# A feed-forward after attention in one 64x64 array shape: contraction halves on two row tiles, one nine steps behind the other

## The chip, the cores and the metric

The kernel runs on one core of one Trainium2 chip. The metric is the time of one execution on the device in microseconds (us), as the median of several executions. Most executions of one kernel agree within about 1%. Every ratio below is the mean time of one kernel's runs over that of the other's runs of the same rounds, so it is not quite the ratio of the medians that are quoted. The span of a profile is about 1.7 us shorter than the time of the same execution.

Names of engines in the profile: PE is the TensorE matmul, PEld its weight load, DVE is VectorE, ACT is ScalarE, POOL is GpSimd, SP is SyncE.

## The reference, cut to what matters

```python
# q, k, v: (8 batches, 12 heads, 448, 64);  w_gate, w_val: (768, 1536);  w_out: (1536, 768)
scores = matmul(q, k.transpose(0, 1, 3, 2)) / sqrt(64)
attn   = maximum(scores, 0) ** 2 / 448
x      = matmul(attn, v)  ->  rows of 768 = 12 heads * 64, for 8 * 448 = 3584 tokens
out    = (maximum(x @ w_gate, 0) * (x @ w_val)) @ w_out         # float32, 3584 x 768
```

## The kernel before

Everything is written as operations with durations; a planner in the kernel orders them on each engine, mixing the attention of batch b+1 into the feed-forward of batch b. Products differ in the shape of the array that they use (a row tile is the part of the array that takes 64 of the contraction's rows, a column tile the part that gives 64 of the output's; a bank is the piece of PSUM, TensorE's output memory, into which one product adds):

- scores: contraction over 64 (the head), 128 keys out, so two heads run at once on two row tiles (64x128), and a rest of 64 keys in four tiles (64x64);
- values: contraction over 128 keys, 64 columns out, two heads at once on two column tiles (128x64), and the rest in four tiles;
- the feed-forward: full array (128x128).

```python
# scores (Part.s): j and h2 pick one of four heads, c a chunk of 128 keys
if not tail:
    for m, j in enumerate(js):
        for h2 in range(2):
            nc.tensor.matmul(half_of(h2)[:, m * n:(m + 1) * n],
                             lhsT=kq(1, j, h2, key_off(b) + c * 128, 128),
                             rhs=kq(0, j, h2, self.c0, n), start=True, stop=True)
else:
    for j, h2, half in ((0, 0, 0), (0, 1, 1), (1, 0, 1), (1, 1, 0)):      # 64x64 each
        ...
# values (Part.pv), after four 64x64 matmuls of the key rest
for j in range(2):
    for c in range(NC):
        for h2 in range(2):
            o = slice(64 * h2, 64 * h2 + 64)
            nc.tensor.matmul(x_of(o, j), lhsT=st.vv[:, 4 * g + 2 * j + h2, 1 + c, :],
                             rhs=self.at(j, c, h2), start=False, stop=(c == NC - 1))
# feed-forward, gate and value products (gv_ops): KD = 6 steps of 448 columns each
for kd in range(KD):
    nc.tensor.matmul(ps, lhsT=w[c][:, kd, o:o + 128], rhs=st.xT[:, kd, cols],
                     start=(kd == 0), stop=(kd == KD - 1))
# feed-forward, output product (ffn_ops): KF = 12 steps of 384 columns
for kf in range(KF):
    nc.tensor.matmul(loc["o"], lhsT=hs["hT"][:, kf, ti * 128:(ti + 1) * 128],
                     rhs=w_out_sb[hf][:, kf, :], start=(kf == 0), stop=(kf == KF - 1))
# attention of batches 1 to 7 goes to the planner in bursts of three products;
# the first product of a burst borrows two of the feed-forward's four PSUM banks (split)
for k0 in (0, NC):
    nb += 1
    for i in range(k0, k0 + NC):
        att.append((pt.s(i, split=i == k0), nb))
nb += 1
att.append((pt.s(pt.tail), nb))
...            # then the value product of the group before, in the same burst
```

Of the kernel before, what the change touches and what calls it, by code (L numbers as in the profile page):

```python
# [14 lines left out]
XBAR_FROM = 2  # L15

# [17 lines left out]
class Op:  # L34
    def __init__(self, engs, emit, deps=(), alloc=(), reads=(), xfer=0.0, prio=1, delay=0.0, bias=0.4):
        self.engs, self.emit = engs, emit
        self.deps, self.alloc, self.reads = list(deps), list(alloc), list(reads)
        self.xfer, self.prio, self.delay = xfer, prio, delay
        self.bias = bias
        self.lat = 1.3  # L40
        self.start = self.end = None


class Planner:
    LAT = 0.26
    NOUT = 8

    def __init__(self):
        self.t = {"POOL": 1.35}
        self.ops = []  # L50
        self.dmaq = 0.0
        self.landed = []

    def ready(self, op):
        r = 0.0
        for d in op.deps:
            if d.end is None:
                return None
            r = max(r, d.end + self.LAT + op.delay)
        need = {}  # L60
        for b in op.alloc:
            need[b.res] = need.get(b.res, 0) + 1
        for res, n in need.items():
            if len(res.free) < n:
                return None
            r = max(r, sorted(res.free)[n - 1] + self.LAT)
        return r
# [12 lines left out]
    def commit(self, op, s, e):  # L80
        op.start, op.eng = s, e
        d = op.engs[e]
        self.t[e] = s + d
        op.end = s + d
        if op.xfer:
            if e == "POOL":
                self.dmaq = max(self.dmaq, op.end + op.lat) + op.xfer
                op.end = self.dmaq + 0.7
                self.landed.append(op.end)
            else:  # L90
                op.end += 2.0 + op.xfer
        for b in op.alloc:
            b.res.free.remove(min(b.res.free))
            b.last = op.end
        for b in op.reads:
            b.readers -= 1
            b.last = max(b.last, op.end)
            if b.readers == 0:
                b.res.free.append(b.last)
        self.ops.append(op)  # L100


def plan(att, ffn, others, pool, nburst, calm):
# [9 lines left out]
    while ai < len(att) or fi < len(ffn) or pend or pi < len(pool):  # L113
# [37 lines left out]
        elif pick == "A":  # L151
# [8 lines left out]
            gap = work / max(1, left) if left > 0 and last_burst >= calm else 0.0  # L160
# [4 lines left out]
    return [P.ops[i] for i in order]  # L165
# [3 lines left out]
def kernel(  # L169
# [19 lines left out]
    P2 = 64  # L189
# [139 lines left out]

    zeros = const.tile([128, 512], BF16)  # L330
# [5 lines left out]
    def transpose_pair(b, g, j):  # L336
# [21 lines left out]
        op = Op({"PE": 0.5 if g or b else 0.95}, emit, deps=list(st.qk_op[h]) + list(st.qk_op[h + 1]) + [id_op],  # L358
# [48 lines left out]
    class Part:  # L407
# [37 lines left out]
        def s(self, i, split=False):  # L445
# [10 lines left out]
            def emit():  # L456
# [9 lines left out]
                if not tail:  # L466
                    for m, j in enumerate(js):
                        for h2 in range(2):
                            nc.tensor.matmul(half_of(h2)[:, m * n:(m + 1) * n],  # L469
                                             lhsT=kq(1, j, h2, key_off(b) + c * 128, 128),  # L470
                                             rhs=kq(0, j, h2, self.c0, n), start=True, stop=True)
                else:

                    for j, h2, half in ((0, 0, 0), (0, 1, 1), (1, 0, 1), (1, 1, 0)):
                        nc.tensor.matmul(half_of(h2)[64 * half:64 * half + 64, :n],  # L475
                                         lhsT=kq(1, j, h2, key_tail(b), P2),
                                         rhs=kq(0, j, h2, self.c0, n), start=True, stop=True)

            op = Op({"PE": (0.06 if not tail else 0.11) + ne / 2400.0}, emit, deps=[t_op[(b, 2 * g + j)] for j in js],
# [29 lines left out]
        def pv(self, split=False):  # L509
            b, g, n = self.b, self.g, self.n  # L510
# [4 lines left out]
            def emit():  # L515
                if split:
                    loc["x"] = [bank("x1_ps"), bank("x1_ps")]
                    x_of = lambda o, j: loc["x"][j][o, :n]
                else:
                    loc["x"] = bank_pair()  # L520
                    x_of = lambda o, j: loc["x"][o, j, :n]
                for j, h2, half in ((0, 0, 0), (0, 1, 1), (1, 0, 1), (1, 1, 0)):
                    p = slice(64 * half, 64 * half + 64)
                    o = slice(64 * h2, 64 * h2 + 64)
                    nc.tensor.matmul(x_of(o, j), lhsT=st.vv[p, 4 * g + 2 * j + h2, (NC + 1) * (1 - half), :],  # L525
                                     rhs=self.at_tail(h2)[p], start=True, stop=False)
                for j in range(2):
                    for c in range(NC):
                        for h2 in range(2):
                            o = slice(64 * h2, 64 * h2 + 64)  # L530
                            nc.tensor.matmul(x_of(o, j), lhsT=st.vv[:, 4 * g + 2 * j + h2, 1 + c, :],  # L531
                                             rhs=self.at(j, c, h2), start=False, stop=(c == NC - 1))

            dv = [d for h in range(4 * g, 4 * g + 4) for d in st.v_op[h]]
            op = Op({"PE": 0.2 + 7 * n / 2400.0}, emit, deps=self.sq + dv, alloc=ps, reads=[self.at_buf, st.vbuf])
# [24 lines left out]
            return op  # L560
# [3 lines left out]
    def gv_ops(b, c0, n, mf):  # L564
# [10 lines left out]
        def product(name, w):  # L575
            ps = bank(name)[:, :n]
            for kd in range(KD):
                nc.tensor.matmul(ps, lhsT=w[c][:, kd, o:o + 128], rhs=st.xT[:, kd, cols],  # L578
                                 start=(kd == 0), stop=(kd == KD - 1))
            loc[name] = ps  # L580

        def emit_relu(op):
            loc["gs"] = gpool.tile([128, S], BF16, name="g_sb")[:, :n]
            if op.eng == "ACT":
                nc.scalar.activation(loc["gs"], loc["g_ps"], AF.Relu)  # L585
            else:
                nc.vector.tensor_scalar_max(loc["gs"], loc["g_ps"], 0.0)

        def emit_mul():
            if "hT" not in hs:  # L590
                hs["hT"] = hpool.tile([128, KF, 2 * S], BF16, name="hT")
            nc.vector.tensor_tensor(hs["hT"][:, mf, t0:t0 + n], loc["v_ps"], loc["gs"], ALU.mult)  # L592

        pe = {"PE": 0.03 + 6 * n / 2400.0}
        ga, va, gs = Buf(r_f, 1), Buf(r_f, 1), Buf(r_g, 1)
        gop = Op(pe, lambda: product("g_ps", w_gate_sb), deps=xop[(b, c0)] + [wg_op[c]], alloc=[ga], reads=[st.x_buf])
        grel = Op(on_psum(n), None, deps=[gop], alloc=[gs], reads=[ga], prio=0)
        grel.emit = lambda: emit_relu(grel)
        vop = Op(pe, lambda: product("v_ps", w_val_sb), deps=xop[(b, c0)] + [wv_op[c]], alloc=[va], reads=[st.x_buf])
        vmul = Op({"DVE": 0.09 + n / 960.0}, emit_mul, deps=[vop, grel], alloc=[hs["buf"]] if first else [],  # L600
                  reads=[va, gs], prio=0)
        hs["mul"].append(vmul)
        others.extend([grel, vmul])
        return [gop, vop]

    def ffn_ops(b):
# [8 lines left out]
        for (c0, n), mf in order:  # L615
            res += gv_ops(b, c0, n, mf)
# [3 lines left out]
        for ti in tiles:  # L620
# [3 lines left out]
            for hf in range(2):  # L624
                loc = {}

                def emit_o(ti=ti, hf=hf, loc=loc, ol=ol):
                    loc["o"] = bank("o_ps")[:, :OH]
                    for kf in range(KF):
                        nc.tensor.matmul(loc["o"], lhsT=hs["hT"][:, kf, ti * 128:(ti + 1) * 128],  # L630
                                         rhs=w_out_sb[hf][:, kf, :], start=(kf == 0), stop=(kf == KF - 1))

                ps = Buf(r_f, 1)
                op = Op({"PE": 1.97}, emit_o, deps=hs["mul"] + [wo_op[hf]], alloc=[ps], reads=[hs["buf"]])
                res.append(op)

                def emit_oc(cp, c0, n, hf=hf, loc=loc, ol=ol):
# [3 lines left out]
                    src = loc["o"][:, c0:c0 + n]  # L641
# [13 lines left out]
                for c0, n, engs in pieces:  # L655
                    cost = {e: d for e, d in on_psum(n).items() if e in engs}
                    cp = Op(cost, None, deps=[op] + cps[:1], alloc=[obuf] if hf == 0 else [], reads=[ps], prio=0)
                    cp.emit = lambda cp=cp, f=emit_oc, c0=c0, n=n: f(cp, c0, n)
                    done.append(cp)
# [82 lines left out]
    def W(n, us):  # L742
        if n:
            att.append((Op({"PE": us}, lambda: idle(n), alloc=[Buf(r_f, 1)]), nb))
# [6 lines left out]
    att.append((Op({"PE": 3.0}, first_zeros), nb))  # L751
# [4 lines left out]
    for x in ORDER.split():  # L756
# [8 lines left out]
        elif x[0] == "V":  # L765
            att.append((part[x[1]][int(x[2])].pv(single), nb))
# [7 lines left out]
    for b in range(1, B):  # L774
        for g in range(NQ):
            pt = Part(b, g, 0, S)
            if b in (XBAR_FROM, XBAR_FROM + 1) and g == 0:

                nb += 1
                att.append((prev.pv(), nb))  # L780
                xburst[prev.b] = nb
                prev = None
            for k0 in (0, NC):
                nb += 1
                for i in range(k0, k0 + NC):
                    att.append((pt.s(i, split=i == k0), nb))
            nb += 1
            att.append((pt.s(pt.tail), nb))
            if prev is not None:
                att.append((prev.pv(), nb))  # L790
                if prev.g == NQ - 1:
                    xburst[prev.b] = nb
            T(b, g + 1)
            prev = pt
    nb += 1
    att.append((prev.pv(), nb))
    xburst[B - 1] = nb
    for b in range(B):
        ffn += [(b, o) for o in ffn_ops(b)]
# [37 lines left out]
```

## Time and profile before

| | before |
|---|---|
| time, median of 3 runs | 437.96 us (437.55 to 439.13) |
| TensorE matmuls busy | 427.1 of 438.1 us |
| VectorE, ScalarE busy | 231.6 and 199.2 us |
| matmuls | 3014, with as many weight loads |
| changes of the array's shape along TensorE's list | 195 |

TensorE is the bound: 98% busy, and 93% of the chain that ended last. But "busy" says only that some matmul is under way. How close it is to pure streaming must be read from the distance between starts. In this trace steps of 384 columns are 162 to 163 ns apart and steps of 448 columns 189 ns, so 64 more columns take about 26.5 ns: 2.4 columns per ns. The timeline of TensorE (start us, length us, engine, line, operation, output<-inputs, array rows*columns, size, count):

```profile
199.67 1.30 PE L578 MATMUL v_ps<-xT,wv_102 128*128 128x448 bf16 x6
200.90 0.38 PE L475 MATMUL s_ps<-qkT 64*64 64x448 bf16 x4
201.11 0.36 PE L525 MATMUL s_ps<-at,vv 64*64 64x448 bf16 x4
201.40 1.32 PE L531 MATMUL s_ps<-at,vv 128*64 128x448 bf16 x12
202.66 1.12 PE L578 MATMUL g_ps<-xT,wg_96 128*128 128x448 bf16 x5
```

In the single records the six matmuls of `v_ps` start 189 ns apart, which is 448 columns at 2.4 per ns (186.7) and 2.4 ns more. The last one starts at 200.613 and the first 64x64 matmul at 200.895: 282 ns, that is 93 ns lost where the shape changes. About the same loss stands ahead of 201.40 and 202.66. The step after a change can be slow as well: the two 64x64 steps at 200.895 and 201.109 are 214 ns apart instead of 189. "Busy" hides it, because a record lasts about 350 ns and covers the gap.

To account for the whole span I cut it into four stages: up to the first feed-forward product (start), until the last output matmul of batch 0 starts (batch-0 stage), until the last matmul starts (chain stage), and the rest (end). The chain stage lasts 352.5 us, of which 332.5 are pure streaming of columns (all columns in it over 2.4 per ns, four 64x64 matmuls counted as one). The 20.0 us beyond that are what a change here can win; 133 changes of shape are most of it (the prediction counts 131 from a slightly later point).

### The profile page before, as it was taken

To read this page: it belongs to the slowest core of one execution; us is meant where nothing else is said; L and a number is where in the kernel's file an instruction comes from. 1 tells how busy PE (TensorE), PEld (TensorE's weight loads), DVE (VectorE), ACT (ScalarE), POOL (GpSimd) and SP (SyncE) were. 2 spreads that over 40 slices of the span, in tenths; PEclk is the share of its full clock that TensorE was granted. 3 is DMA by queue.
4 is the path that set the end of the run, shared out by engine and by line. 5 is a ranking of instruction groups with operands and counts; after the bars stand their busy time and mean duration, and the time that the engine had idled before them with its cause. 6 is when DMAs were issued, how large, how long until landed. Compare 5 with 4: busy or idle time off the path is not lost.

```text
span 438.1 us, 7425 instructions
## 1 busy us (share of the span) xinstructions
PE 427.1 (98%) x3014; PEld 224.9 (51%) x3014; DVE 231.6 (53%) x411; ACT 199.2 (45%) x340; POOL 46.2 (11%) x72
## 2 busy tenths in 40 slices
PE   6799999999999999999999999999999999999996
PEld 2577775544454444444455444554445444555553
DVE  3787787167734776674644656545653456202210
ACT  2575555344644454553553554444544444332221
POOL 8536210010002002000200200010000000000000
PEclk9689999999999999999999999999999999999999
DMA  7999999982189647918956990990002200040014
GB/s 104 192 198 198 202 202 188 143 138 46 17 145 199 110 69 101 228 37 126 143 91 105 167 162 3 135 171 1 1 1 76 71 0 2 4 105 0 1 36 108
DMA packets 75170, 44.12 MB, mean 101 GB/s; under 512 B 34560, under 2 KB 71680, under 8 KB 75136
## 3 DMA queue, kind: packets, MB, share of 16 engines
q0 software_dynamic: 37856, 24.38, 39.2%
q1 hardware_dynamic: 37200, 19.17, 22.6%
q8 instruction: 23, 0.38, 0.4%
q10 hardware_dynamic: 80, 0.10, 0.1%
q14 instruction: 11, 0.09, 0.1%
HBM read 48.76 MB, written 11.01 MB: 136 GB/s over the span
## 4 chain that ended last, share of the span: by engine, by line
PE 93%; DMA 4%; POOL 1%; issue 0%; DVE 0%; SPq 0%; ACT 0%; POOLq 0%
PE o_ps L630 25%; PE g_ps L578 25%; PE v_ps L578 25%; PE s_ps L469 7%; PE s_ps L531 6%; DMA qkT<-spare 2%; DMA qk<-in_q_dram 2%; PE s_ps L475 2%; PE x_ps L531 1%; PE s_ps L525 1%; POOL qk L246 1%; PE t_ps L346 1%; PE x_ps L525 0%; POOL vv L246 0%; DVE qkT L355 0%
## 5 line engine op out<-in xcount | busy, mean ns | idle before, releaser
L485 ACT ACTIVATE r_sb<-s_ps 128x896 bf16<-128x896 f32 (+4 forms) x146 | 99.6, 736 | 37.3 <-PE s_ps L469 25.8
L592 DVE TENSOR_TENSOR hT<-v_ps,g_sb 128x448 bf16<-128x448 f32 (+2 forms) x108 | 61.5, 570 | 102.0 <-PE v_ps L578 101.9
L503 DVE TENSOR_TENSOR at<-r_sb 128x896 bf16<-128x896 bf16 (+4 forms) x163 | 93.6, 612 | 22.8 <-ACT r_sb L485 22.6
L585 ACT ACTIVATE g_sb<-g_ps 128x448 bf16<-128x448 f32 (+2 forms) x106 | 53.6, 506 | 110.9 <-PE g_ps L578 108.1
L487 DVE TENSOR_SCALAR r_sb<-s_ps 128x448 bf16<-128x448 f32 (+5 forms) x72 | 62.5, 898 | 50.7 <-PE s_ps L469 50.5
L630 PEld LDWEIGHTS <-hT 128*128 128x128 bf16 x672 | 64.0, 98 | 48.7 <-issue 8.0
L643 ACT ACTIVATE o_sb<-o_ps 128x384 f32<-128x384 f32 (+1 forms) x56 | 27.3, 488 | 71.7 <-PE o_ps L630 71.7
L630 PE MATMUL o_ps<-wo_106,hT 128*128 128x384 bf16 x336 | 59.4, 327 | 0.0
L630 PE MATMUL o_ps<-wo_107,hT 128*128 128x384 bf16 x336 | 59.2, 326 | 0.0
L469 PE MATMUL s_ps<-qkT 64*128 64x448 bf16 (+2 forms) x324 | 38.0, 341 | 1.4 <-DVE qkT L355 1.1
L531 PE MATMUL s_ps<-at,vv 128*64 128x448 bf16 x252 | 27.8, 357 | 0.0
L547 ACT CAST xT<-s_ps 128x896 bf16<-128x896 f32 (+1 forms) x22 | 19.6, 891 | 12.7 <-PE s_ps L531 12.7
L531 PEld LDWEIGHTS <-vv 128*64 128x64 bf16 x324 | 16.7, 115 | 14.5 <-issue 7.7
L469 PEld LDWEIGHTS <-qkT 64*128 64x128 bf16 x324 | 11.8, 96 | 22.4 <-issue 15.6
L578 PE MATMUL g_ps<-xT,wg_94 128*128 128x448 bf16 (+2 forms) x108 | 21.4, 332 | 0.1
L578 PE MATMUL g_ps<-xT,wg_96 128*128 128x448 bf16 (+2 forms) x108 | 21.2, 332 | 0.0
L578 PE MATMUL g_ps<-xT,wg_99 128*128 128x448 bf16 (+2 forms) x108 | 21.2, 332 | 0.0
L578 PE MATMUL g_ps<-xT,wg_97 128*128 128x448 bf16 (+2 forms) x108 | 21.2, 332 | 0.0
L578 PE MATMUL v_ps<-xT,wv_102 128*128 128x448 bf16 (+2 forms) x108 | 21.2, 332 | 0.0
L578 PE MATMUL v_ps<-xT,wv_101 128*128 128x448 bf16 (+2 forms) x108 | 21.2, 332 | 0.0
L578 PE MATMUL g_ps<-xT,wg_98 128*128 128x448 bf16 (+2 forms) x108 | 21.2, 332 | 0.0
L578 PE MATMUL g_ps<-xT,wg_95 128*128 128x448 bf16 (+2 forms) x108 | 21.2, 332 | 0.0
(63 smaller groups left out, 333.5 us busy)
## 6 DMA issues: line engine op xcount, KB each, us to landing
out_dram<-o_sb SPq DMA_DIRECT2D x54, 192.0 KB, 2.7
vv<-in_v_dram POOLq DMA_DIRECT2D x12, 384.0 KB, 12.2
qk<-in_k_dram POOLq DMA_DIRECT2D x6, 672.0 KB, 7.1
qk<-in_q_dram POOLq DMA_DIRECT2D x6, 672.0 KB, 9.8
wo_106<-in_moe_w_out_dram POOLq DMA_DIRECT2D x1, 1152.0 KB, 15.4
wo_107<-in_moe_w_out_dram POOLq DMA_DIRECT2D x1, 1152.0 KB, 20.3
qk<-in_k_dram POOLq DMA_DIRECT2D x5, 224.0 KB, 10.5
qk<-in_q_dram POOLq DMA_DIRECT2D x5, 224.0 KB, 9.5
```

Source lines behind the costliest of these rows:

```text
L469: nc.tensor.matmul(half_of(h2)[:, m * n:(m + 1) * n], lhsT=kq(1, j, h2, key_off(b) + c * 128, 128), rhs=kq(0, j, h2, self.c0, n), start=Tr ...
L475: nc.tensor.matmul(half_of(h2)[64 * half:64 * half + 64, :n], lhsT=kq(1, j, h2, key_tail(b), P2), rhs=kq(0, j, h2, self.c0, n), start=True ...
L485: nc.scalar.activation(dst, src, AF.Relu)
L487: nc.vector.tensor_scalar_max(dst, src, 0.0)
L503: lambda: nc.vector.tensor_tensor(self.at_tile(i), loc["r"][:, :2 * ne], loc["r"][:, :2 * ne], ALU.mult),
L531: nc.tensor.matmul(x_of(o, j), lhsT=st.vv[:, 4 * g + 2 * j + h2, 1 + c, :], rhs=self.at(j, c, h2), start=False, stop=(c == NC - 1))
L547: nc.scalar.copy(dst, src)
L578: nc.tensor.matmul(ps, lhsT=w[c][:, kd, o:o + 128], rhs=st.xT[:, kd, cols], start=(kd == 0), stop=(kd == KD - 1))
L585: nc.scalar.activation(loc["gs"], loc["g_ps"], AF.Relu)
L592: nc.vector.tensor_tensor(hs["hT"][:, mf, t0:t0 + n], loc["v_ps"], loc["gs"], ALU.mult)
L630: nc.tensor.matmul(loc["o"], lhsT=hs["hT"][:, kf, ti * 128:(ti + 1) * 128], rhs=w_out_sb[hf][:, kf, :], start=(kf == 0), stop=(kf == KF - 1))
L643: nc.scalar.activation(out=dst, in_=src, func=AF.Copy, scale=float(out_scale))
```

## The change

The intent: from batch 1 on, every product is made of 64x64 matmuls, so that the shape never changes. A 128-row contraction is then two halves on the two row tiles. Both halves add into the same PSUM bank, and the Trainium skill (TensorEngine Tiling, Gotcha 1: PSUM Pressure) says that different row tiles cannot access one bank at the same time. So the lower row tile follows nine steps behind the upper one, where that is on another bank, and a semaphore wait guards each hand-over of a bank. The value product is treated alike: first each row tile on its own pair of heads, then swapped. Batch 0's feed-forward stays in the full array.

The diff, cut to its core:

```diff
+LAG = 9
+CHUNK = 6
@@ scores
-                            nc.tensor.matmul(half_of(h2)[:, m * n:(m + 1) * n],
-                                             lhsT=kq(1, j, h2, key_off(b) + c * 128, 128),
+                            for o in (0, P2):
+                                nc.tensor.matmul(half_of(h2)[o:o + P2, m * n:(m + 1) * n],
+                                                 lhsT=kq(1, j, h2, key_off(b) + c * 128 + o, P2),
@@ values: two operations, xo (each row tile on its own j) and, later, op (swapped)
+            def fours(cs, swap):
+                for c in cs:
+                    for row in range(2):
+                        j = row ^ swap
+                        p = slice(64 * row, 64 * row + 64)
+                        for h2 in range(2):
+                            ...
+            def emit_x():
+                loc["last"] = fours([NC] + list(range(NC)), 0)
+            def emit_y():
+                ordered(loc["last"])                  # wait for the row tiles' own work
+                fours(range(NC), 1)
@@ feed-forward: one step of a product on one row tile
+        def piece(self, row, k):
+            ...
+            if row == 0 and k == 0:
+                self.bank = bank(self.name)
+            elif k % CHUNK == 0:
+                ordered(self.last[1 - row])
+            for col in range(2):
+                c = slice(64 * col, 64 * col + 64)
+                ins = nc.tensor.matmul(self.out()[c], lhsT=self.weights(p, k)[:, c], rhs=self.moving(p, k), ...)
@@ the chain: the upper row tile at step t, the lower at step t - LAG; products of 12 steps
@@ go in groups of 3 or 4: first halves of all, then second halves of all
+        for c in range(0, n + LAG, six):
+            top = [slots[t] if t < n else None for t in range(c, c + six)]
+            low = [slots[t - LAG] if 0 <= t - LAG < n else None for t in range(c, c + six)]
+            ...
@@ attention of batches 1 to 7: every product is a burst of its own, no borrowed banks
-            for k0 in (0, NC):
-                nb += 1
-                for i in range(k0, k0 + NC):
-                    att.append((pt.s(i, split=i == k0), nb))
+            for o in mine:
+                nb += 1
+                att.append((o, nb))
@@
+    ffn = full_ops([x for x in prods if x.b == 0]) + chain_ops([x for x in prods if x.b > 0])
```

## The prediction

> **What bounds the kernel.** TensorE. The page gives matmuls busy 427.1 of 438.1 us (98%), VectorE 53%, ScalarE 45%; the chain of waits is 93% TensorE. The table of windows shows TensorE idle only in the first 35 us and the last 4, so only its own stream matters.
>
> In the timeline's single records, 448-column steps in one mode start 189 ns apart (2.4 ns over pure streaming); two-column-tile (128x64) steps too. Where the tile shape changes, the next start comes 280 to 290 ns after: about 0.10 us lost. The Trainium skill (TensorEngine Tiling, Key Properties) says that a mode switch drains TensorE; this trace agrees. I count 195 shape changes: 131 after batch 0's feed-forward ends (82 us), 41 during it, 23 before. From 82 us on, starts exceed pure streaming by 19.7 us, of which the 131 changes are 13.3.
>
> **What the change does** (counts from the instruction order of both builds).
> - Removes: shape changes after batch 0's feed-forward go 131 to 1: -12.9 us net. The slow first step after a change (213 instead of 189 ns for column tiles) goes too: -1.0.
> - Adds: batch 0's feed-forward stays full-array while attention comes in single products: 41 to 67 changes there, +2.6 us.
> - Adds: the nine-step lag leaves two of four tiles idle for 9 steps at each end of the chain (1.6 us lost), and pairs 384- with 448-column steps at batch borders (up to 1.5 us more).
> - Moves: matmuls 3014 to 8414, with as many weight loads; eight instructions per step of 162 to 189 ns, 20 to 24 ns each. The densest stretches of before reach 19 ns over 80 instructions, 25 over 128, so this rate held continuously is not shown. A 64-column weight load takes 103 to 110 ns (98 the full one), under a step, and four start within 10 ns. I take 190 ns per step: +1 us.
> - Semaphore waits between row tiles look back mostly four to five steps, 650 ns or more; a matmul record lasts 352 ns, so they should be met.
> - Banks: feed-forward slack between last write and reuse is 1.7 to 1.9 us, as the tightest before (1.9). Score/value pairs lose their helper banks: 11 reuses come within 1.0 to 1.1 us of a value product whose eviction takes 0.9 us plus latencies. I allow +2 us of stalls.
>
> **Sum.** -13.9 + 2.6 + 3.1 + 1 + 2, less about 1.5 us if row tiles slip past each other at the borders: about -6.5, all on the critical path.
>
> Predicted 431.3 us, range 425 to 439. Chances: faster by over 2% 0.33, within 2% 0.59, slower by over 2% 0.08.
>
> **What would show it.** From 85 to 430 us the timeline has only 64*64 matmuls, step starts 189 to 191 ns apart (448) and 162 to 164 (384), no 100 ns gaps at attention. Longer steps throughout (195 ns or more) would mean that instruction issue, weight loads or concurrent accumulation limit, and cost 9 us per 5 ns. Weight loads waiting on matmuls would show the lag too short. Idle before score matmuls, released by ScalarE or VectorE, would show bank stalls; busy VectorE and ScalarE times should stay within 2%. Batch 0's stretch up to about 85 us should lengthen by 2 to 3 us.
>
> **What would make it wrong.** A four-tile pace that differs from two tiles' (before has only isolated pairs of four-tile steps, 207 to 214 ns apart right after a change); bank stalls larger than allowed; a lower granted clock.

## More of the kernel before

Batch 0 is cut into two parts of 192 and 256 tokens, so its feed-forward steps are shorter: 192 or 256 columns in gate and value products.

The page of the profile, lines of its parts on engines, DMA queues and the chain of waits (engine, busy us, share of the span, instructions; queue, packets, MB, share):

```profile
span 438.1 us, 7425 instructions
PE 427.1 (98%) x3014; PEld 224.9 (51%) x3014; DVE 231.6 (53%) x411; ACT 199.2 (45%) x340; POOL 46.2 (11%) x72
q8 instruction: 23, 0.38, 0.4%
PE 93%; DMA 4%; POOL 1%; issue 0%; DVE 0%; SPq 0%; ACT 0%; POOLq 0%
```

## The result, and the profile after

The changed kernel took 431.66 us in the median (4 runs, 429.8 to 433.33) against 438.12 us (4 runs) before: ratio 0.9854, 95% interval 0.9822 to 0.9886. That is 6.5 us faster, inside 2%, as predicted.

The same lines of the page:

```profile
span 431.6 us, 18155 instructions
PE 418.6 (97%) x8414; PEld 364.2 (84%) x8414; DVE 185.5 (43%) x346; ACT 241.8 (56%) x363; POOL 46.3 (11%) x72
q8 instruction: 66, 1.08, 1.0%
PE 92%; DMA 4%; POOL 1%; issue 0%; ACT 0%; SPq 0%; DVE 0%; POOLq 0%
```

TensorE is the bound as before. VectorE gave 46 us of work to ScalarE: the planner moved evictions, which the prediction had excluded, and it did no harm. The queue `q8`, which fetches instructions, made 66 fetches of 16 KB instead of 23; this will matter below.

The timeline, in the same place as before:

```profile
201.27 0.38 PE L642 MATMUL g_ps<-xT,wg 64*64 64x448 bf16 x2
201.38 0.35 PE L642 MATMUL v_ps<-xT,wv 64*64 64x448 bf16 x2
201.46 0.84 PE L550 MATMUL s_ps<-at,vv 64*64 64x448 bf16 x12
202.03 0.84 PE L642 MATMUL g_ps<-xT,wg 64*64 64x448 bf16 x12
```

The value product (`s_ps`) comes in without a gap: the matmuls of one row tile (the lower) start at 201.269, 201.458, 201.647 in the single records, 189 ns apart across the border between feed-forward and attention. The two row tiles need not start together: the upper one starts its steps here 110 ns after the lower. They drift further where the chain goes from the value products of a batch to its output products, because the upper tile then streams 384 columns a step while the lower, nine steps behind, still streams 448:

```profile
120.46 0.49 PE L642 MATMUL o_ps<-wo,hT 64*64 64x384 bf16 x4
120.62 0.35 PE L642 MATMUL v_ps<-xT,wv 64*64 64x448 bf16 x2
120.78 0.33 PE L642 MATMUL o_ps<-wo,hT 64*64 64x384 bf16 x2
120.81 0.35 PE L642 MATMUL v_ps<-xT,wv 64*64 64x448 bf16 x2
```

The `o_ps` matmuls start 162 to 163 ns apart (120.456, 120.619, 120.781) and the `v_ps` matmuls 189 (120.623, 120.812). TensorE's list has them strictly by turns, two `o_ps`, two `v_ps`; at 120.456 to 120.622 four `o_ps` start in a row, and by 120.944 an `o_ps` starts 57 ns ahead of a `v_ps` (121.001) that stands before it. The upper tile overtakes the lower.

By stages, in the two traces:

| stage | before, us | after, us | streaming, before / after | beyond streaming, before / after |
|---|---|---|---|---|
| start | 24.9 | 25.7 | | |
| batch 0 | 56.1 | 60.6 | 50.7 / 51.4 | 5.4 / 9.1 |
| chain | 352.5 | 340.2 | 332.5 / 331.8 | 20.0 / 8.4 |
| end | 4.6 | 5.2 | | |

The chain stage wins 11.6 us of what is beyond streaming, the batch-0 stage loses 3.7, and the start and the end are longer by 0.8 and 0.6. The start varies from run to run: over the traces of all kernels here that keep the changed kernel's start, the first product began between 21.9 and 26.2 us, with 0.85 to 1.00 of the clock granted over the first 35 us. I did not study why. Single spans therefore differ by up to 4 us for a reason outside the change, and I compare stages of traces, and times only over several runs.

Most of the 8.4 us left in the chain stage is accounted for: 4.3 are the ordinary 2.3 ns of each of 1862 steps per tile, about 1.5 are the last nine steps of the lower row tile alone, and 1.7 are four places where the whole array stood still: two short waits at the very beginning of the stage, of 0.42 us (for ScalarE's copy of x) and 0.51 (for batch 2's transposed heads), of which before has counterparts of 0.3 us each, and two of 0.58 and 0.18 us with no semaphore in front. The larger of these two, in the timeline:

```profile
182.09 1.14 PE L642 MATMUL o_ps<-wo,hT 64*64 64x384 bf16 x22
183.64 0.35 PE L642 MATMUL o_ps<-wo,hT 64*64 64x384 bf16 x2 [0.42 <-issue]
```

"issue" is the profile's word for an engine that waited for nothing that is recorded.

### The profile page after: what moved, and what is told of

Same layout as the page of the kernel before. It is cut to its first block, busy times and chain, and to the rows that moved or that the text cites. A ratio compares the mean times of both kernels' runs of the same rounds, so it can differ in the third digit from the quotient of the medians.

```text
span 431.6 us, 18155 instructions
## 1 busy us (share of the span) xinstructions
PE 418.6 (97%) x8414; PEld 364.2 (84%) x8414; DVE 185.5 (43%) x346; ACT 241.8 (56%) x363; POOL 46.3 (11%) x72
## 4 chain that ended last, share of the span: by engine, by line
PE 92%; DMA 4%; POOL 1%; issue 0%; ACT 0%; SPq 0%; DVE 0%; POOLq 0%
PE o_ps L642 23%; PE v_ps L642 22%; PE g_ps L642 22%; PE s_ps L494 7%; PE s_ps L550 6%; PE v_ps L632 4%; PE g_ps L632 3%; DMA qkT<-spare 2%; PE o_ps L632 2%; DMA qk<-in_q_dram 2%; PE s_ps L501 1%; PE x_ps L575 1%; PE t_ps L370 1%; POOL qk L265 1%; POOL vv L265 0%
## 5 line engine op out<-in xcount | busy, mean ns | idle before, releaser
L511 ACT ACTIVATE r_sb<-s_ps 128x896 bf16<-128x896 f32 (+4 forms) x169 | 150.2, 895 | 73.4 <-PE s_ps L494 58.8
L642 PE MATMUL g_ps<-xT,wg 64*64 64x448 bf16 x2016 | 183.6, 349 | 0.3 <-ACT xT L596 0.3
L642 PE MATMUL v_ps<-xT,wv 64*64 64x448 bf16 x2016 | 176.5, 349 | 0.0
L642 PE MATMUL o_ps<-wo,hT 64*64 64x384 bf16 x2400 | 126.0, 323 | 0.4 <-issue 0.4
L642 PEld LDWEIGHTS <-wg 64*64 64x64 bf16 x2016 | 113.1, 107 | 5.4 <-issue 0.5
L642 PEld LDWEIGHTS <-wv 64*64 64x64 bf16 x2016 | 113.0, 107 | 5.3
L642 PEld LDWEIGHTS <-hT 64*64 64x64 bf16 x2400 | 101.4, 107 | 12.1 <-issue 1.2
L494 PE MATMUL s_ps<-qkT 64*64 64x448 bf16 (+2 forms) x648 | 66.8, 341 | 2.4 <-DVE qkT L379 1.1
L494 PEld LDWEIGHTS <-qkT 64*64 64x64 bf16 x648 | 30.9, 109 | 10.9 <-issue 6.1
L550 PE MATMUL s_ps<-at,vv 64*64 64x448 bf16 x588 | 39.6, 350 | 0.0
L632 PEld LDWEIGHTS <-wv 128*128 128x128 bf16 x144 | 11.6, 98 | 4.7 <-issue 4.0
```

Of the source, the lines that this page charges most:

```text
L494: nc.tensor.matmul(half_of(h2)[o:o + P2, m * n:(m + 1) * n], lhsT=kq(1, j, h2, key_off(b) + c * 128 + o, P2), rhs=kq(0, j, h2, self.c0, n) ...
L511: nc.scalar.activation(dst, src, AF.Relu)
L550: ins = nc.tensor.matmul(x_of(slice(64 * h2, 64 * h2 + 64), j), lhsT=st.vv[p, 4 * g + 2 * j + h2, (NC + 1) * (1 - row) if tail else 1 + c, :],
L632: nc.tensor.matmul(self.out(), lhsT=self.weights(p, k), rhs=self.moving(p, k), start=(k == 0), stop=(k == self.nk - 1))
L642: ins = nc.tensor.matmul(self.out()[c], lhsT=self.weights(p, k)[:, c], rhs=self.moving(p, k), start=(row == 0 and k == 0), stop=(row == 1 ...
```

## The experiments

Theory A: the gain is the drain at each change of shape, about 0.10 us each. Rival B: it comes from attention being handed over in single, evenly spread products. Rival C: it comes from the two row tiles slipping past each other, which packs the array better. Two more questions: whether nine steps of lag are needed and harmless, and what the stops without a releaser are.

### Feed-forward back in the full array

```diff
-    ffn = full_ops([x for x in prods if x.b == 0]) + chain_ops([x for x in prods if x.b > 0])
+    ffn = full_ops(prods)
```

> The changed kernel with its attention in 64x64 tiles and in its new order, but every feed-forward product in the full array again. Shape changes rise from 87 to 374 (counted in the build). Theory A (what the change saves is the drain at each shape change, 0.10 us net each): 287 more changes cost 28 us, the lag's half-filled steps (about 1.6 us) go, so about 458 us, and each change shows 95 to 130 ns beyond its columns. Rival B (what helps is attention in single products spread evenly, not the uniform shape): it keeps that order, so it should stay below before's 438 us.

Measured: 470.0 us (4 runs), ratio to before 1.0729 (1.0699 to 1.0758). Rival B falls: with the new order of attention but mixed shapes the kernel is 7% slower than before. Theory A has the right sign and a size that is too small by 12 us. The timeline shows the gap on either side of a score product (the starts 300.89 and 301.21 are 320 ns apart, for 448 columns):

```profile
300.89 0.38 PE L494 MATMUL s_ps<-qkT 64*64 64x448 bf16 x4
301.21 2.12 PE L632 MATMUL o_ps<-wo,hT 128*128 128x384 bf16 x12
```

In the chain stage 143 changes into four tiles cost a median of 96 ns, and 143 back into the full array cost 129 ns, not 0.10 us: 32 us together at those medians. (Costs of a change are counted here from the first start of the last step before it, less that step's columns.) The 129 ns are a change and a slow step in one: after a four-tile product of a single step the way back costs a median of 129 ns (110 of the changes), after one of two steps or more 105 ns (the others). The 24 ns between are the slow first step after a change, which in a product of one step can only show up there. The one large rest is a single wait of 4.0 us at 257.3 us, where a value product waited for ScalarE:

```profile
257.27 1.71 PE L550 MATMUL s_ps<-at,vv 64*64 64x448 bf16 x16 [4.01 <-ACT r_sb L511]
```

Together these explain 36 of the 38.5 us by which this chain stage (378.7 us) is longer than the changed kernel's. From 257.3 to 262.6 us, after that wait, the granted clock was 0.50, which by an estimate (half of the 5.4 us) cost 2.7 us more.

### Attention back in its old shapes

```diff
-                            for o in (0, P2):
-                                nc.tensor.matmul(half_of(h2)[o:o + P2, m * n:(m + 1) * n],
-                                                 lhsT=kq(1, j, h2, key_off(b) + c * 128 + o, P2),
+                            nc.tensor.matmul(half_of(h2)[:, m * n:(m + 1) * n],
+                                             lhsT=kq(1, j, h2, key_off(b) + c * 128, 128),
                                              rhs=kq(0, j, h2, self.c0, n), start=True, stop=True)
...
-            if not self.full:
-                xo, op = None, whole           # value product in 128x64, after four 64x64
+            xo, op = None, whole
...
```

> The changed kernel with its feed-forward chain on two row tiles, but attention in the 64x128 and 128x64 shapes of before. Shape changes 324 against 87. Theory A: 237 more changes at 0.10 us, about 455 us. Rival C (row tiles that slip past each other pack the array better, and the chain alone gives the gain): near the changed kernel's 432 us.

Measured: 457.92 us (4 runs), ratio 1.0439 (1.0400 to 1.0478), with the chain stage 25.6 us longer than the changed kernel's. The four kinds of changes in it (98, 98, 18 and 18 of them) add up to about 24.2 us beyond streaming, 0.104 us each; the slow first steps after them add to this (187 instead of 162 ns after 301.33 below). Rival C falls: the chain on two row tiles is worth nothing while attention still changes the shape. In the timeline of this kernel four matmuls of a 64x128 score product are two steps, 373 ns of streaming, but the next feed-forward matmul starts 490 ns after the product, and the gap before the product is hidden in the same way:

```profile
300.84 0.55 PE L493 MATMUL s_ps<-qkT 64*128 64x448 bf16 x4
301.33 1.17 PE L640 MATMUL o_ps<-wo,hT 64*64 64x384 bf16 x24
```

The two experiments together: neither half of the change gains anything alone. Only the uniform shape does.

### A lag of seven, and of twelve

```diff
-LAG = 9
+LAG = 7        # or 12
```

> Lag of seven steps instead of nine, nothing else. The waits of one row tile for the other then look back mostly 9 or 13 matmuls (2.25 steps, about 425 ns) instead of 17 or 21 (800 ns); a matmul record lasts 350 ns and a weight load 107 ns must follow it. If the lag is there to hide these waits, most of some 230 waits cost about 0.1 us: 445 to 455 us, and gaps of that size stand before weight loads of feed-forward products. If the waits don't matter: 431 to 432 us.

Measured: 432.8 us (4 runs), ratio 0.9874 (0.9837 to 0.9912), the same as nine steps within noise; its chain stage is 340.0 us against 340.2. My expectation of 445 to 455 us was wrong. The records say why: of 104 weight loads whose wait looks back nine matmuls, the earliest starts 384 ns after the matmul that it waits for and the median 411 ns, which is 34 and 61 ns after that record's end (350 ns). In 69 of the 104 the load starts 163 ns into the 189 ns step of its own row tile, only 26 ns before its own matmul, and that matmul still starts on time, though the load's record lasts over 100 ns. I had reckoned as if the load had to come a whole step early. Why it need not isn't shown here.

> Lag of twelve steps. The waits look back 29 matmuls or more, but each bank is held three steps (0.5 us) longer. If at nine steps waits still cost something: faster by 1 us or more. If banks limit instead: slower by 2 to 8 us, with idle before first matmuls of products, released by ScalarE or VectorE. If neither: plus 0.5 us (six more half-filled steps).

Measured: 436.88 us (4 runs), ratio 0.9963 (0.9924 to 1.0002), so nearly all of the gain is gone; the chain stage is 343.8 us. The size is in my range for "banks limit", but the cause is another. The list of waits of this kernel (who waited, for whom, us in total, times, longest) has a line that the changed kernel's has not:

```profile
PEld L642 <- PE o_ps L642: 5.9, 17, 0.4
```

The waiting tile is the upper one. In a group of three output products it begins the second half of the first product 18 steps after its first half, and the lower tile finishes that first half only at 12 + 6 steps. 17 waits look back one or five matmuls, which I had missed: I had counted only the waits of the lower tile. Before output products the array stood still 18 times, 2.2 us in all, and for 0.9 us once more without a releaser. So the lag has room on the short side and hardly any on the long side: with groups of three and chunks of six steps, nine is not a compromise between two costs that were felt, but seven and nine are free and twelve is too long (the lags between were not run).

### Fewer changes in batch 0's stage

The stage lost 3.7 us. In it the changes of shape rose from 39 to 67, since each attention product now comes alone into a feed-forward that is still in the full array. The next experiment hands batch 1's attention over in pairs, changing nothing later:

```diff
-            for o in mine:
-                nb += 1
+            for n_o, o in enumerate(mine):
+                if b > 1 or n_o % 2 == 0:
+                    nb += 1
                 att.append((o, nb))
```

The changed kernel was run again beside it:

> The changed kernel again, five rounds, as the base for its neighbours on the same chip: 430 to 433 us, with the same scatter of about 0.8% (before: 0.4%). In its first trace TensorE stood still for 0.34 and 0.74 us at two places where no semaphore is waited for, both at the same place modulo 256 in TensorE's list of instructions, which is one 16 KB fetch of 64-byte instructions. If instruction fetch causes them, stalls without a releaser stand at that same place modulo 256 again, in the stretch of busy DMA queues (95 to 185 us), though not at the same two fetches; if they have another cause their places modulo 256 are scattered.

(The 0.34 and 0.74 us in it are distances between starts; less the 0.16 us of a step's columns they are the 0.18 and 0.58 us above.)

> The changed kernel with batch 1's attention products (those that fall into batch 0's full-array feed-forward) planned in pairs instead of singly. Shape changes 69 instead of 87, all the difference in that stretch. Theory A: 1.8 us faster, about 429.9 us, with that stretch shorter by as much. If the stretch's extra time came from something else (helper banks, the planner's order), no gain.

Measured, with the same runs of before: the changed kernel 430.43 us (6 runs), ratio 0.9843 (0.9810 to 0.9877); pairs 428.21 us (6 runs), ratio 0.9780 (0.9750 to 0.9811). The stage is 59.2 us long instead of 60.9 in these two traces and holds 0.6 us more attention columns. What is beyond streaming in it fell by 2.0 us: 18 changes fewer, and every change from four tiles back into the full array now follows two steps or more and costs 105 ns (median of 19) instead of 129. Theory A's 1.8 us fits. A second run of pairs, with a lag of seven beside it:

> The pairs of batch 1 again, as base for the next run on the same chip: 427 to 430 us, ratio to before 0.976 to 0.981. Stalls without a releaser, if any, at places 180 to 187 modulo 256 of TensorE's list.

> Pairs of batch 1, and a lag of seven steps. The lag-7 trace showed waited-for weight loads starting 380 ns after the matmul that they wait for, within a step's spare time, and the shorter lag saves four half-filled steps (0.35 us) and holds banks 0.4 us less: 0 to 1 us faster than pairs alone, about 428 us. If the waits do cost something, 1 us or more slower.

Measured: pairs 430.27 us, ratio 0.9802 (0.9768 to 0.9837); pairs with a lag of seven 429.07 us, ratio 0.9794 (0.9766 to 0.9821), 6 runs each. The intervals of pairs and of the plain changed kernel overlap a little over the two jobs, so the gain of about 2 us is likely rather than certain from the times; the stage lengths (59.2, 59.5 and 59.2 us in the three traces with pairs, 60.6 and 60.9 in the two without) show it. Pairs with lag seven had the least scatter (428.6 to 430.9 us) and is the version that I would keep: about 2% faster than before.

### What the stops without a releaser are

A further step along Theory A moves batch 0's six output products into the chain as well:

```diff
+    wide = [x for x in prods if x.b == 0 and x.nk == CHUNK]
+    ffn = full_ops(wide) + chain_ops(prods[len(wide):])
```

> As b1_pairs, and batch 0's six output products (384 columns) join the chain. Shape changes 59. Theory A: 2.8 us faster than the changed kernel, about 428.9 us.

Measured: 434.36 us (6 runs, one of them not fast; 431.95 to 438.83), ratio 0.9915 (0.9878 to 0.9952): slower than pairs alone, against Theory A. The batch-0 stage is as with pairs (59.3 us), but the chain stage is 344.1 us instead of 338.7. The traced run was the fastest of the six (431.95 us), so what the others lost beyond it isn't seen. The chain stage of the trace has a wait of 1.5 us for batch 2's transposed heads (89.2 us), three short stops without a wait (0.75, 0.31 and 0.28 us, at places 184, 181 and 180 in the count explained below), and one long stop, in the timeline here, and the table of windows (stretch, its length, busy time of PE, PEld, DVE, ACT and POOL, granted clock, DMA share, GB/s) shows what follows it:

```profile
286.30 0.60 PE L642 MATMUL g_ps<-xT,wg 64*64 64x448 bf16 x8 [2.52 <-issue]
```

and the windows around it:

```profile
283.00:287.00 4.00, 1.49 (x28) 0.71 (x22) 0.63 (x1) 1.19 (x3) 0.00 (x0) 0.96 1.20 238
287.00:290.00 3.00, 3.00 (x36) 1.55 (x32) 0.62 (x1) 0.47 (x1) 0.00 (x0) 0.50 0.60 214
```

TensorE starts nothing for 2.7 us beyond the end of its stream, and then runs at half the granted clock (0.50) for about 3 us, with 36 matmuls where 63 would fit. The Trainium skill (Runtime: NRT & Kernel Launch, Terms) says of an engine's instruction memory that it is "refilled in 16 KiB blocks". This trace agrees: the `q8` packets are of 16,384 bytes, and there is one for each 256 of TensorE's weight loads and matmuls (66 for 16,828). The stop at 286.3 us stands at place 180 modulo 256 in TensorE's sequence of loads and matmuls. In the changed kernel the unexplained stops stand at 183 and 181, in its second run at 183, with lag 7 at 183 and 181, with lag 12 at 181. In the chain stages of those four traces no other stop of over 0.14 us is without a wait in front of it, and one that has one belongs here too: in the second run 0.25 us at 247.0 us, place 180, where the transfer that is waited for had ended at 221.7 us. (I had expected the second run's stops at other fetches, between 95 and 185 us; the first, at 125.8 us, is at the same fetch as in the first trace, the other is later.) The packets of `q8` settle what these places are: at all of these stops, the packet fetched last ended 1.3 to 1.7 us before the stop did (1.34 and 1.65 us in the changed kernel). They are the boundaries of fetched blocks, where the next block had not come. In `both` the packet of the long stop began only 6.1 us after TensorE had passed the boundary before (277.9 us), with 148 GB/s moved meanwhile; why so late is open.

The strongest test makes TensorE's instructions denser while the DMA queues are full, by putting all of batch 0 into four tiles:

```diff
-    ffn = full_ops([x for x in prods if x.b == 0]) + chain_ops([x for x in prods if x.b > 0])
+    ffn = chain_ops(prods)
```

> All of batch 0's feed-forward in 64x64 tiles too, products of 192 and 256 columns included. Shape changes 28 instead of 87. Theory A alone: 5.8 us faster, about 426 us. Rival D (instruction supply limits short steps: eight instructions per 82 ns step are 10 ns each, against 13 ns in the densest 32 of before, and a 16 KB fetch would be used up in 2.6 to 3.5 us while DMA is busiest): steps of 192 columns come 100 ns or more apart and there are long stalls without a releaser in the first 80 us, so that it gains little or loses, 430 to 445 us.

Measured: 446.97 us (6 runs), ratio 1.0209 (1.0172 to 1.0245). Theory A alone would have given a gain of 6 us; rival D holds, though not in the form that I gave it. The steps themselves are not slow: between stops, 192 and 256 columns still step at 82 and 109 ns, which is eight instructions in 82 ns. What limits most is the supply of blocks: six late blocks between 32 and 76 us stop the array for 10.7 us in all. Not all of the loss is theirs: some 4 us more are waits for ScalarE and VectorE between 35 and 60 us, of which the changed kernel has none there. The stops of over 1 us between 48 and 78 us in the timeline:

```profile
51.42 0.29 PE L642 MATMUL v_ps<-xT,wv 64*64 64x256 bf16 x1 [1.46 <-issue]
57.34 0.27 PE L642 MATMUL g_ps<-xT,wg 64*64 64x192 bf16 x1 [2.00 <-issue]
63.36 0.27 PE L642 MATMUL g_ps<-xT,wg 64*64 64x192 bf16 x2 [1.68 <-issue]
69.28 0.35 PE L642 MATMUL v_ps<-xT,wv 64*64 64x192 bf16 x6 [2.31 <-issue]
75.48 0.38 PE L642 MATMUL g_ps<-xT,wg 64*64 64x256 bf16 x5 [1.12 <-issue]
```

They are 6 us apart, 256 instructions each. The packet of each block began 3.0 us (the first) and 3.6 to 3.8 us (the others) after TensorE had passed the boundary before, took 1.0 us, and the first instruction of the block started 1.3 to 1.5 us later. The last experiment asks whether that delay is fixed or is made by traffic. Batch 2's loads wait here until batch 1's transposes are through; TensorE's instructions stay the same in number and kind:

```diff
+        if b == 2:
+            gate(1, [])
+            late_gate = pool_ops[-1]
...
+    late_gate.deps = [t_op[(1, hp)] for hp in range(HP)]
```

> All of batch 0's feed-forward in 64x64 tiles as in all_chain, the same number of TensorE instructions, but batch 2's loads (about 4 MB) wait until batch 1's transposes are through, so that the DMA queues fall quiet from about 55 us on instead of 74. In all_chain five stalls of 1.3 to 2.5 us without a releaser stood at 51, 57, 63, 69 and 75 us, each at place 185 to 187 modulo 256, after 16 KB instruction fetches that began 3.6 to 3.9 us after the list had passed the last such place. If traffic on the DMA queues delays the fetch: the fetches of the quiet time begin within about 1 us, and the stalls there are gone; those before it stay. If 256 instructions need 6 us whatever the queues do, the stalls stay at 6 us spacing. The total is no test: batch 2's attention comes later.

Measured: 448.44 us (2 runs; the total is no test here). The windows, in the same columns, first of all_chain:

```profile
63.00:77.00 14.00, 10.21 (x305) 9.57 (x308) 4.93 (x10) 6.24 (x10) 0.00 (x0) 0.88 1.07 163
```

then with the gate:

```profile
63.00:77.00 14.00, 12.47 (x428) 11.46 (x428) 7.24 (x15) 8.66 (x14) 0.00 (x0) 1.00 0.07 13
```

and the stops with the gate:

```profile
52.00 0.29 PE L642 MATMUL v_ps<-xT,wv 64*64 64x256 bf16 x1 [1.06 <-issue]
58.19 0.27 PE L642 MATMUL g_ps<-xT,wg 64*64 64x192 bf16 x1 [2.27 <-issue]
64.21 0.27 PE L642 MATMUL g_ps<-xT,wg 64*64 64x192 bf16 x2 [1.68 <-issue]
71.39 0.38 PE L642 MATMUL g_ps<-xT,wg 64*64 64x256 bf16 x5 [0.21 <-issue]
```

The queues fell quiet at about 63.5 us (13 GB/s instead of 163). The fetches after that began 1.1 us after the boundary instead of 3.7, blocks followed each other every 3.5 to 3.8 us instead of 6, TensorE ran 428 matmuls in the 14 us instead of 305, and the stops after 64.5 us went from 2.3 and 1.1 us to a single one of 0.2. When traffic came back later in this run, so did a long stop: 2.5 us at 303.1 us, at place 181, after a packet that began 6.2 us after the boundary, with 143 GB/s moved meanwhile. So traffic on the DMA queues delays the refill of TensorE's instructions, and a stream of 64x64 matmuls uses 256 instructions in 5.2 to 6.05 us (384 and 448 columns), which is just what the refill gave under full traffic in all_chain (6 us a block). That leaves the changed kernel without reserve. The traces of the changed kernel and its neighbours lost 0.4 to 1.0 us to late blocks in the chain stage, and `both` 4.0 us besides the half clock; that this is a matter of where boundaries fall against the loads is likely but not shown.

## Why the prediction was right, point by point

- The total (431.3 predicted, 431.66 measured) and the main cause are right: TensorE's own stream, and the drains at changes of shape. Both halves of the 2x2 (full_ffn, mixed_att) confirm it. That it came out within 0.4 us is luck: the chain stage did 2.3 us better than the sum said, batch 0's stage 1.1 us worse, and the start and the end, which the sum left out, took 1.4 us more in these two traces; single runs of the changed kernel differ by 3.5 us.
- The chain stage: predicted -13.9 us from drains and slow first steps, +3.1 - 1.5 for the lag and the batch borders, +1 for the pace, +2 for stalls, so -9.3. Measured: -11.6. The pace cost nothing (189 ns a step and a median of 2.3 ns beyond streaming, as before). The stalls are 1.7 us, about 1.1 more than before.
- "Less about 1.5 us if row tiles slip past each other at the borders" is right as to the mechanism: they do where widths of 384 and 448 meet, as the timeline at 120.5 us shows. What it saved alone was not measured.
- "41 to 67 changes there, +2.6 us" was mis-sized. Beyond streaming the stage lost 3.7 us. The count was right; the price was not: changes from four tiles back into the full array cost 129 ns (median of 27 in this stage, 143 in full_ffn), where I had taken 100 for all. The part that I left out is the slow first step, which I had counted among the changes that go (213 instead of 189 ns) but not among those that come: most of the added products have one step only. The profile of before had that pair of shapes five times, and I had averaged over it.
- "Semaphore waits between row tiles ... should be met" is right, with more room than I thought (lag 7). What I had not seen is that the lag is limited from above by the upper tile's waits in groups of three (lag 12).
- "11 reuses come within 1.0 to 1.1 us of a value product ... I allow +2 us of stalls" failed as a step. None of the four stops of the chain stage is such a reuse. The size of the allowance was met by something else: two waits that before has too, and late instruction blocks. I had looked at the rate of instructions ("20 to 24 ns each ... not shown") as a limit on issue. Issue can do more (8 instructions in 82 ns in all_chain); the limit is the refill of whole blocks.
- "Busy VectorE and ScalarE times should stay within 2%" is wrong: 231.6 to 185.5 and 199.2 to 241.8 us. The planner chooses the engine of an eviction by its own clock, and with other times it chose otherwise. It cost nothing.

What stays open: how often the late blocks strike in runs without a profile. Only traced executions show them, one for each kernel.

## What to carry to other kernels

When TensorE is "98% busy", measure the distance between starts against columns over the clock: a gap of 0.1 us at each change of array shape hides under records that last 0.35 us. A uniform shape pays only when nothing is left that changes it; either half of this change alone made the kernel 4 to 7% slower than before. Smaller tiles multiply instructions, and instructions come in blocks by DMA, which the data's traffic delays: before cutting matmuls finer, compare the time in which TensorE uses 256 of them with the time that a refill takes while the loads run.

## What the Trainium skill lacked or had wrong

- TensorEngine Tiling (Key Properties) says that a change of tiling mode drains TensorE but gives no cost. Here, beyond the columns: 96 to 98 ns from and to the full array with 64x128 tiles and into 64x64, 105 ns between 64x64 and 64x128, 105 ns from 64x64 to the full array, and 129 where the 64x64 product had one step only (medians). The first step after a change can be some 24 ns slow (213 or 214 instead of 189 ns).
- TensorE: Matmul & The Clock Gate (Part 3, The mechanism) says that matmuls start and end in the order of the program, without reordering. Here a 384-column matmul of the upper row tile started at 120.944 us, 57 ns ahead of a 448-column matmul of the lower row tile (121.001 us) that stands before it in the list; within a tile the order held. A kernel that lets one semaphore on the last matmul stand for several row tiles should not rest on the order of the list; no run here tests that.
- The same page (Part 1, the two states) puts the return to half clock after an idle window of about 3.4 us. In the kernel `both` a stop of 2.7 us was followed by 3.4 us at a granted clock of 0.50; in all_chain_gated a stop of 2.4 us (at 58.2 us) was not.
- Runtime: NRT & Kernel Launch (Terms) gives the 16 KiB blocks of instruction refill, but no page gives the time: the packet began 1.1 us after the boundary with quiet queues and mostly 3.6 to 3.8 us after it under about 200 GB/s (6.1 us once in `both`, 6.2 once in all_chain_gated, under about 145 GB/s), took about 1 us, and the block's first instruction started some 1.4 us later.
- TensorE: Matmul & The Clock Gate (Part 3, The mechanism) says in one bullet that weight loads overlap running matmuls only when the row group differs, while a paragraph above it also lets loads into the background weight buffer go ahead. The bullet is too strict: in before, a full-array weight load for the next matmul began 2 ns after the start of a full-array matmul (199.858 and 199.856 us) and took 98 of the step's 189 ns, and with a lag of seven loads that had waited started 26 ns before their own matmul, which still came on time.
